# First-layer weights: two VectorE operations a tile through PSUM, the low word's bits from ScalarE

## The chip, the cores and the metric

The kernel runs on one core of one Trainium2 chip. The metric is the device time of one execution in microseconds; less is better. The engines have short names in all rows: PE is TensorE's matmuls, PEld its weight loads, DVE is VectorE, ACT ScalarE, POOL GpSimd, SP SyncE (which here only issues DMAs).

## The reference

Attention in two parts (a pooled one over groups of four positions, and a local band), then two feed-forward layers over 2304 tokens of 512. The layers' weights arrive as 64-bit floats; q, k and v as 32-bit ones.

```python
def _attn_ref(q, k, v):                      # 4 batches, 8 heads, 576 positions, 64 wide
    q_d = q.reshape(B, H, Sd, factor, D).mean(axis=3)
    ...
    out_d = sm_attn(q_d, k_d, v_d)
    out_up = np.repeat(out_d, factor, axis=2)
    mask = np.abs(pos[:, None] - pos[None, :]) < factor
    ...
    return out_up + out_local

def _moe_ref(x, w_in, w_out):                # w_in 512 x 2048, w_out 2048 x 512
    h = x @ w_in
    g = np.where(h > 0.0, h, np.exp(np.minimum(h, 0.0)) - 1.0)
    return g @ w_out

def _moe2_ref(x, w_gate, w_val, w_out):      # 1536 wide
    g = x @ w_gate
    silu = g * (1.0 / (1.0 + np.exp(-g)))
    return silu * (x @ w_val) @ w_out
```

## The kernel before

A planner inside the kernel (class Work) orders everything: each piece of work is a task with an engine, a cost, a due time, the tiles that it reads and writes, and optional earlier tasks (after). When an engine is free in the planner's clock, it takes the ready task that is due first and whose tiles have room. What comes out is one fixed queue for each engine; on the chip each engine works through its queue in order and waits where a semaphore isn't set. So costs and due times move the order, not the chip's durations.

The first layer runs over eight chunks of 288 tokens (T1), three attention units of 96 positions each; batch b fills chunks 2b and 2b+1. In a chunk there are 16 steps f: gemm1 (x by w_in's column block f) into bank 6 or 7, an activation that gives g, and gemm2 (g by w_out's row block f) into banks 0 to 3. Chunk 0 (add_whole, L702) multiplies in plain f32: L713 is gemm1, L718 gemm2 (in the trace the four matmuls of one of these products are eight rows), ScalarE makes e at L723 and L724, VectorE g at L725. Chunks 1 to 7 use split weights and activations, each as a high and a low part in a faster format, three products for each (L688 to L690), with e and g at L757 to L768.

The weights come as pairs of 32-bit words of 64-bit floats. A tile is 128 partitions by 512 numbers, 512 KB of raw words (load_w); the first layer has 32 of them, w_in and w_out for each f. add_words (L341) makes 32-bit floats u of them:

- size (L344, ScalarE): the high word, read as f32, times a power of two, into u. That brings the exponent to the narrower format.
- words_a (L348, VectorE): u shifted left by three bits.
- words_b (L352 and L354, VectorE): the sign bit of the high word or-ed into u, then the low word shifted right by 29 or-ed into u.

The same three steps serve the second layer's weights (add_weights_away), in halves of 256 columns that pass through the tile mid and are written back to DRAM (wd), from the end of chunk 0 on. add_weight_split (L392) makes the two parts for chunks 1 to 7: a cast on ScalarE or VectorE (copy, L275 and L277), then the difference on GpSimd (L400).

Attention for batch 0 runs before chunk 0, for batches 1 to 3 beside the chunks ahead of those that need them. A unit (add_unit) transposes q and k on TensorE (L474), takes scores (L501), a softmax on VectorE, ScalarE and GpSimd, and values (L555); add_pooled does the pooled part of a batch in four pieces (praw are its rows of v, summed at L578 and L579); add_split puts both together as x (L666 to L676). Attention takes its PSUM banks from att_bank: any of the eight at first, and only 4 and 5 once the first layer's products have begun.

All tiles of weights share 33 places of SBUF: raw words in places 19 to 32, u in halves of places 0 to 18, split weights in any that is free. So a raw tile is loaded when a place is free.

Of the kernel before, what the change touches and what calls it, by code (L numbers as in the profile page):

```python
# [9 lines left out]
F32 = mybir.dt.float32  # L10
F32R = mybir.dt.float32r
BF16 = mybir.dt.bfloat16
I32 = mybir.dt.int32
AF = mybir.ActivationFunctionType
ALU = mybir.AluOpType
X = mybir.AxisListType.X
# [2 lines left out]
P = 128  # L19
# [10 lines left out]
UPC = 3  # L30
# [26 lines left out]
class Half(Buf):  # L57
# [5 lines left out]
    t = property(lambda self: False if self.whole.t is None else self.whole.t[:, self.i])  # L63
# [56 lines left out]
class Work:  # L120
# [18 lines left out]
    def add(self, engine, cost, due, fn, reads=(), writes=(), after=(), nbytes=0, second=None, slack=0.0):  # L139
        t = self.Task()  # L140
        t.slack = slack
        t.costs = {engine: cost} if isinstance(engine, str) else dict(zip(engine, cost))
        t.due, t.fn, t.nbytes = due, fn, nbytes
        t.bufs = list(dict.fromkeys([*reads, *writes]))
        t.next, t.left = [], 0
        for d in dict.fromkeys([*after, *(w for b in reads for w in b.writers)]):
            d.next.append(t)
            t.left += 1
        for b in t.bufs:
            b.left += 1  # L150
        for b in writes:
            b.writers.append(t)
        self.made += 1
        second = self.SECOND if second is None else second
        t.key = {e: (t.due + i * second * ("act" in t.costs), self.made) for i, e in enumerate(t.costs)}
        for e in t.costs:
            self.ready.setdefault(e, [])
        if not t.left:
            self.offer(t)
        return t  # L160
# [67 lines left out]
def attention_moe_moe(ctx: ExitStack, tc: tile.TileContext, q, k, v, w_in, w_out, w_gate, w_val, w_o2, ident_in, mask_in, band_in, picks_in, out):  # L228
    nc = tc.nc
# [5 lines left out]
    NF1, NF2 = FF1 // P, FF2 // P  # L235
    HALF = G // 2
    scale = 1.0 / float(D) ** 0.5
    NU = S // U
# [9 lines left out]
    NW = 2 * NF1 + 1  # L248
    U0, U1 = 6, 19
# [35 lines left out]
    add = work.add  # L285
# [3 lines left out]
    w_raws = Places(lambda i: pairs(pools["w"].tile([P, 1024], I32, tag=f"w{i}", name="w")), NW)  # L289
# [4 lines left out]
    begun = []  # L294
    banks = Places(lambda i: pools["ps"].tile([P, 512], F32, tag=f"bank{i}", name="bank"), 8)

    def att_bank():
        return banks.new(lambda: [4, 5] if begun else [4, 5, 6, 0, 1, 2, 3, 7])

    def bank(*places):  # L300
        return banks.new(lambda: places)
# [5 lines left out]
    EAGER, URGENT, SLACK = 15.0, 14.0, 1.0  # L307
# [13 lines left out]
    BIAS = (1023 - 127) // 8  # L321
# [19 lines left out]
    def add_words(due, raw, u, reads=()):  # L341

        def size():
            nc.scalar.mul(u.t.bitcast(F32), raw.t[:, :, 1].bitcast(F32), 2.0 ** -BIAS)  # L344

        def words_a():
            t = u.t.bitcast(I32)
            nc.vector.tensor_scalar(out=t, in0=t, scalar1=3, scalar2=None, op0=ALU.logical_shift_left)  # L348

        def words_b():  # L350
            t = u.t.bitcast(I32)
            nc.vector.scalar_tensor_tensor(  # L352
                out=t, in0=raw.t[:, :, 1], scalar=-0x80000000, op0=ALU.bitwise_and, in1=t, op1=ALU.bitwise_or)
            nc.vector.scalar_tensor_tensor(  # L354
                out=t, in0=raw.t[:, :, 0], scalar=29, op0=ALU.logical_shift_right, in1=t, op1=ALU.bitwise_or)

        part = 0.5 if isinstance(raw.room, Places) and raw.room is not w_raws else 1.0
        add("act", 0.69 * part, due - 4, size, reads=[raw, *reads], writes=[u])
        add("dve", 0.6 * part, due - 3, words_a, reads=[u], writes=[u])
        return add("dve", 1.8 * part, due - 2.5, words_b, reads=[raw, u], writes=[u])  # L360

    def add_weights(keys, dues, whole):

        made = {}
        for n, key in enumerate(keys):
            raw, w = w_raws.new(lambda: range(NW - 1, U1 - 1, -1)), whole(n)
            add("sp", 0.5, dues[n] - 36.0, lambda key=key, raw=raw: load_w(key, raw.t), writes=[raw], nbytes=P * 4096)
            made[key] = add_words(dues[n], raw, w, [w.whole])
            ww[key] = w
        return made  # L370

# [69 lines left out]

    sums = {}

    def add_unit(n, due, load_due, rows=None, after=()):

        b, i = divmod(n, NU)
        q0 = i * U
# [21 lines left out]
        for which, t, dst, count, start, own in ((0, tq, qT, U, 0, 0), (1, tk, kT, KU, PAD, off)):  # L469
            pt = att_bank()  # L470

            def turn(t=t, count=count, pt=pt):
                for p in range(NP):
                    nc.tensor.transpose(pt.t[:, p * count:(p + 1) * count], t.t[:count, p * P:(p + 1) * P], ident[:count, :count])  # L474

            def keep(engine, dst=dst, count=count, start=start, pt=pt):
                copy(engine, dst.t[:, :, start:start + count], pt.t[:, :NP * count].rearrange("p (a t) -> p a t", a=NP))

            half = half_ring.new()

            def pool(engine, which=which, dst=dst, own=own, half=half):
                x = dst.t[:, :, own:own + U].rearrange("p a (g r) -> p a g r", r=R)
                to = sums[b].t[:, which, :, i * GU:(i + 1) * GU]
                if engine == "dve":
                    nc.vector.tensor_reduce(out=to, in_=x, op=ALU.add, axis=X)
                else:
                    nc.gpsimd.tensor_tensor(out=half.t, in0=x[:, :, :, :2], in1=x[:, :, :, 2:], op=ALU.add)
                    nc.gpsimd.tensor_tensor(out=to, in0=half.t[:, :, :, 0], in1=half.t[:, :, :, 1], op=ALU.add)

            add("pe", 0.4, due - EAGER, turn, reads=[t], writes=[pt, dst], slack=SLACK)  # L490
            add(COPIER, (0.5, 0.55), due + 1, keep, reads=[pt], writes=[dst], second=1)
            add(EITHER, (0.56, 1.1), due + 2, pool, reads=[dst], writes=[sums[b], half])

        sc = [att_bank(), att_bank()]

        def scores():
            for p in range(NP):
# [359 lines left out]
    with tc.manual_schedule():  # L857
# [33 lines left out]

        xfs = {}
        for n in range(NU):
            xfs[n] = add_unit(n, 4.0 * n, -40 + 2 * n, rows=(*rows[n], vals[n]))
            if n == 0:
                load_mask()
        for p in range(NP):
# [16 lines left out]
        for b in range(1, B):  # L914
            lo, hi = (time1(s) for s in spans[b])
            for i in range(NU):
                due = lo + (hi - lo) * i / NU
                xfs[b * NU + i] = add_unit(b * NU + i, due, due - 18, after=[words["in", 10 if b == 1 else NF1 - 1]])
            for p in range(NP):
                add_pooled(b, p, hi + 2 * p, hi - 20 + 2 * p)  # L920
            while split < (b + 1) * NU and split // UPC < NC:
                if split // NU == b or xdT[split // NU] is not None:
                    made += [add_split(split, xfs[split], time1(NF1 * (split // UPC)) - 12.0)]
                split += 1
# [70 lines left out]
```

## Time and profile before

| | us |
|---|---|
| median of 3 runs (lowest, highest) | 1056.06 (1055.63, 1056.79) |
| profiled execution, its own time | 1057.0 |
| profiled execution, span | 1055.2 |
| TensorE busy | 1003.8 (95%) |
| VectorE busy | 547.3 (52%) |
| ScalarE busy | 395.6 (37%) |
| GpSimd busy | 344.9 (33%) |

The profiled execution is one run with the hardware profiler on; its own time is the span and 1.8 us around it, and 0.94 us above the median. Shares are means over the whole span: the 95% of TensorE hold for a kernel with a front part (attention and chunk 0, up to about 165 us) and a long part of split products.

### The profile page before, as it was taken

What the parts mean: (1) busy time and instruction counts of PE and PEld (TensorE: products, weight loads), DVE (VectorE), ACT (ScalarE), POOL (GpSimd) and SP (SyncE); (2) the same over time, 40 slices, a digit from 0 to 9 for tenths busy, and PEclk for the clock granted to TensorE, in tenths of its full rate; (3) what the DMA queues carried; (4) which work ended last, traced back from release to release, by engine and by line L of the source; (5) the groups of instructions that cost most, each with busy time, mean ns of one, the idle gap of its engine ahead of it and who ended that gap; (6) DMA issues with size and microseconds to landing.
All of it is one profiled execution on the core that took longest, in us unless ns stands there. A gap on an engine that the chain in (4) does not pass through costs nothing. (4 is left out here: it accounts for less than half of the span.)

```text
span 1055.2 us, 19383 instructions
## 1 busy us (share of the span) xinstructions
PE 1003.8 (95%) x7540; PEld 869.6 (82%) x7540; DVE 547.3 (52%) x1088; ACT 395.6 (37%) x972; POOL 344.9 (33%) x390
## 2 busy tenths in 40 slices
PE   7768979999999999999999999999999999999998
PEld 4556758989999899899998888888888888888897
DVE  4899998886787877873123422222223222222232
ACT  4553546555555465555343531121112111211121
POOL 4475685373344634347347830010001000100000
PEclk7569989999999999999999999999999999999999
DMA  9966516455554476433114420011002000100010
GB/s 155 279 214 185 124 30 154 116 146 150 147 148 122 131 193 160 119 84 100 33 34 129 140 73 21 1 41 41 1 1 65 6 1 1 50 1 1 1 40 21
DMA packets 129004, 91.20 MB, mean 86 GB/s; under 512 B 73744, under 2 KB 116880, under 8 KB 128912
## 3 DMA queue, kind: packets, MB, share of 16 engines
q1 hardware_dynamic: 128768, 89.70, 31.6%
q8 instruction: 59, 0.97, 0.4%
q14 instruction: 33, 0.27, 0.1%
q10 hardware_dynamic: 144, 0.26, 0.1%
HBM read 71.06 MB, written 18.87 MB: 85 GB/s over the span
## 5 line engine op out<-in xcount | busy, mean ns | idle before, releaser
L688 PE MATMUL bank<-x,w 128*128 128x288 f32 (+2 forms) x928 | 317.0, 342 | 8.4 <-DVE e L761 8.3
L689 PE MATMUL bank<-x,w 128*128 128x288 f32 (+2 forms) x928 | 310.9, 335 | 0.1
L690 PE MATMUL bank<-x,w 128*128 128x288 f32 (+2 forms) x928 | 309.9, 334 | 0.0
L834 DVE TENSOR_TENSOR e<-bank,e 128x512 f32<-128x512 f32 (+1 forms) x120 | 76.2, 637 | 260.8 <-ACT e L831 179.3
L688 PEld LDWEIGHTS bank<-x,w 128*128 128x128 f32 x928 | 174.3, 188 | 32.7 <-DVE e L761 12.3
L689 PEld LDWEIGHTS bank<-x,w 128*128 128x128 f32 x928 | 174.9, 188 | 17.0 <-POOL x L676 0.3
L690 PEld LDWEIGHTS bank<-x,w 128*128 128x128 f32 x928 | 174.7, 188 | 16.8
L768 POOL TENSOR_TENSOR g<-e,g 128x288 fp32r<-128x288 f32 x112 | 94.0, 840 | 167.7 <-ACT g L275 117.0
L688 PE MATMUL bank<-g,w 128*128 128x288 f32 x448 | 134.9, 301 | 1.6 <-DVE o L277 1.6
L689 PE MATMUL bank<-g,w 128*128 128x288 f32 x448 | 132.2, 295 | 0.0
L690 PE MATMUL bank<-g,w 128*128 128x288 f32 x448 | 131.9, 294 | 0.0
L811 POOL TENSOR_TENSOR x<-x2r,x 128x512 fp32r<-128x512 f32 (+1 forms) x20 | 23.5, 1193 | 270.2 <-ACT x L810 270.2
L831 ACT ACTIVATE e<-bank 128x512 f32<-128x512 f32 (+1 forms) x60 | 33.2, 556 | 190.3 <-PE bank L690 190.3
L836 ACT CAST y<-e 128x512 fp32r<-128x512 f32 (+1 forms) x60 | 34.6, 577 | 154.9 <-DVE e L834 132.9
L761 DVE SCALAR_TENSOR_TENSOR e<-e,bank 128x288 f32<-128x288 f32 x112 | 50.3, 449 | 76.0 <-ACT e L765 66.2
L688 PEld LDWEIGHTS bank<-g,w 128*128 128x128 f32 x448 | 84.1, 188 | 4.1 <-DVE o L277 1.9
L689 PE MATMUL bank<-w,y 128*128 128x512 f32 x216 | 85.7, 397 | 0.0
L688 PE MATMUL bank<-w,y 128*128 128x512 f32 x216 | 85.3, 395 | 0.0
L690 PE MATMUL bank<-w,y 128*128 128x512 f32 x216 | 84.9, 393 | 0.0
L689 PEld LDWEIGHTS bank<-g,w 128*128 128x128 f32 x448 | 84.6, 189 | 0.2
L690 PEld LDWEIGHTS bank<-g,w 128*128 128x128 f32 x448 | 84.5, 189 | 0.0
L757 ACT ACTIVATE e<-bank 128x288 f32<-128x288 f32 x112 | 46.1, 411 | 99.3 <-PE bank L690 73.0
(114 smaller groups left out, 1458.8 us busy)
## 6 DMA issues: line engine op xcount, KB each, us to landing
wd<-mid SPq DMA_DIRECT2D x72, 128.0 KB
u<-wd SPq DMA_DIRECT2D x36, 256.0 KB
w<-in_moe_w_in_dram SPq DMA_DIRECT2D x16, 512.0 KB
w<-in_moe_w_out_dram SPq DMA_DIRECT2D x16, 512.0 KB
w<-in_moe_w_gate_dram SPq DMA_DIRECT2D x24, 256.0 KB
w<-in_moe_w_val_dram SPq DMA_DIRECT2D x24, 256.0 KB
w<-in_moe_w_out_dram SPq DMA_DIRECT2D x24, 256.0 KB
out_dram<-x2r SPq DMA_DIRECT2D x17, 256.0 KB
```

Of the source, the lines that this page charges most:

```text
L688: nc.tensor.matmul(ps, sh, mh, start=first, stop=False)
L689: nc.tensor.matmul(ps, sh, ml, start=False, stop=False)
L690: nc.tensor.matmul(ps, sl, mh, start=False, stop=last)
L757: nc.scalar.activation(e.t, h.t[:, :T1], AF.Relu, scale=-1.0)
L761: nc.vector.scalar_tensor_tensor(out=e.t, in0=e.t, scalar=-1.0, op0=ALU.add, in1=h.t[:, :T1], op1=ALU.max)
L768: add("pool", 0.82, due - URGENT, lambda e=e, g=g: nc.gpsimd.tensor_tensor(out=g.t[:, 1], in0=e.t, in1=g.t[:, 0], op=ALU.subtract), reads= ...
L811: add("pool", 1.3, due, lambda T=T, raw=raw, x=x: nc.gpsimd.tensor_tensor(out=x.t[:, 1, :T], in0=raw.t[:, :T], in1=x.t[:, 0, :T], op=ALU.s ...
L831: add("act", 0.6, due, lambda T=T, e=e, gate=gate: nc.scalar.activation(e.t[:, :T], gate.t[:, :T], AF.Sigmoid), reads=[gate], writes=[e], ...
L834: add("dve", 0.64, due, lambda T=T, e=e, x=x: nc.vector.tensor_tensor(out=e.t[:, :T], in0=x.t[:, :T], in1=e.t[:, :T], op=ALU.mult), reads= ...
L836: add("act", 0.6, due, lambda T=T, e=e, y=y: nc.scalar.copy(y.t[:, 0, :T], e.t[:, :T]), reads=[e], writes=[y])
```

## The change

The first layer's weights no longer go through add_words. add_weights has its own three functions. ScalarE does two operations a tile: rest (L377 of the changed kernel) makes the low word's top three bits, by reading it as an unsigned number, scaling it by 2 to the minus 29 with an offset, and converting to an integer in u; size (L374) writes the scaled high word into a PSUM bank, 4 or 5. VectorE does two: L381 shifts the bank's content left by three and ors the low bits in, in the bank; L383 takes the sign from the high word and ors the bank in, into u.

With that go changes to the order. Attention before chunk 0 has banks 6, 0, 1, 2, 3 and 7 and leaves 4 and 5. Units 4 to 6 of batch 0 (those of chunk 1) have everything behind their transposes due 24 us later in the planner (late). The transposes of batches 1 to 3 wait until the last word tile is done (then). The planner's costs for word operations are changed too: add_words, now for halves only, and the new tasks.

```diff
--- before.py
+++ after.py
@@ -11,6 +11,7 @@
 F32R = mybir.dt.float32r
 BF16 = mybir.dt.bfloat16
 I32 = mybir.dt.int32
+U32 = mybir.dt.uint32
 AF = mybir.ActivationFunctionType
 ALU = mybir.AluOpType
 X = mybir.AxisListType.X
@@ -295,7 +296,7 @@
     banks = Places(lambda i: pools["ps"].tile([P, 512], F32, tag=f"bank{i}", name="bank"), 8)
 
     def att_bank():
-        return banks.new(lambda: [4, 5] if begun else [4, 5, 6, 0, 1, 2, 3, 7])
+        return banks.new(lambda: [4, 5] if begun else [6, 0, 1, 2, 3, 7])
 
     def bank(*places):
         return banks.new(lambda: places)
@@ -354,18 +355,38 @@
             nc.vector.scalar_tensor_tensor(
                 out=t, in0=raw.t[:, :, 0], scalar=29, op0=ALU.logical_shift_right, in1=t, op1=ALU.bitwise_or)
 
-        part = 0.5 if isinstance(raw.room, Places) and raw.room is not w_raws else 1.0
-        add("act", 0.69 * part, due - 4, size, reads=[raw, *reads], writes=[u])
-        add("dve", 0.6 * part, due - 3, words_a, reads=[u], writes=[u])
-        return add("dve", 1.8 * part, due - 2.5, words_b, reads=[raw, u], writes=[u])
+        add("act", 0.36, due - 4, size, reads=[raw, *reads], writes=[u])
+        add("dve", 0.33, due - 3, words_a, reads=[u], writes=[u])
+        return add("dve", 1.0, due - 2.5, words_b, reads=[raw, u], writes=[u])
+
+
+
+    TOP3 = 2.0 ** -29 * (1 - 2.0 ** -20), -0.5 + 2.0 ** -18
 
     def add_weights(keys, dues, whole):
 
         made = {}
         for n, key in enumerate(keys):
-            raw, w = w_raws.new(lambda: range(NW - 1, U1 - 1, -1)), whole(n)
-            add("sp", 0.5, dues[n] - 36.0, lambda key=key, raw=raw: load_w(key, raw.t), writes=[raw], nbytes=P * 4096)
-            made[key] = add_words(dues[n], raw, w, [w.whole])
+            raw, w, ps = w_raws.new(lambda: range(NW - 1, U1 - 1, -1)), whole(n), bank(4, 5)
+            due = dues[n]
+
+            def size(raw=raw, ps=ps):
+                nc.scalar.mul(ps.t, raw.t[:, :, 1].bitcast(F32), 2.0 ** -BIAS)
+
+            def rest(raw=raw, w=w):
+                nc.scalar.activation(w.t.bitcast(I32), raw.t[:, :, 0].bitcast(U32), AF.Copy, bias=TOP3[1], scale=TOP3[0])
+
+            def words(raw=raw, w=w, ps=ps):
+                t, p = w.t.bitcast(I32), ps.t.bitcast(I32)
+                nc.vector.scalar_tensor_tensor(
+                    out=p, in0=p, scalar=3, op0=ALU.logical_shift_left, in1=t, op1=ALU.bitwise_or)
+                nc.vector.scalar_tensor_tensor(
+                    out=t, in0=raw.t[:, :, 1], scalar=-0x80000000, op0=ALU.bitwise_and, in1=p, op1=ALU.bitwise_or)
+
+            add("sp", 0.5, due - 36.0, lambda key=key, raw=raw: load_w(key, raw.t), writes=[raw], nbytes=P * 4096)
+            add("act", 0.69, due - 4, rest, reads=[raw, w.whole], writes=[w])
+            add("act", 0.69, due - 3.5, size, reads=[raw], writes=[ps])
+            made[key] = add("dve", 1.5, due - 2.5, words, reads=[raw, w, ps], writes=[w, ps])
             ww[key] = w
         return made
 
@@ -441,7 +462,7 @@
 
     sums = {}
 
-    def add_unit(n, due, load_due, rows=None, after=()):
+    def add_unit(n, due, load_due, rows=None, after=(), then=(), late=0.0):
 
         b, i = divmod(n, NU)
         q0 = i * U
@@ -487,11 +508,12 @@
                     nc.gpsimd.tensor_tensor(out=half.t, in0=x[:, :, :, :2], in1=x[:, :, :, 2:], op=ALU.add)
                     nc.gpsimd.tensor_tensor(out=to, in0=half.t[:, :, :, 0], in1=half.t[:, :, :, 1], op=ALU.add)
 
-            add("pe", 0.4, due - EAGER, turn, reads=[t], writes=[pt, dst], slack=SLACK)
+            add("pe", 0.4, due - EAGER, turn, reads=[t], writes=[pt, dst], slack=SLACK, after=then)
             add(COPIER, (0.5, 0.55), due + 1, keep, reads=[pt], writes=[dst], second=1)
             add(EITHER, (0.56, 1.1), due + 2, pool, reads=[dst], writes=[sums[b], half])
 
         sc = [att_bank(), att_bank()]
+        due += late
 
         def scores():
             for p in range(NP):
@@ -891,7 +913,7 @@
 
         xfs = {}
         for n in range(NU):
-            xfs[n] = add_unit(n, 4.0 * n, -40 + 2 * n, rows=(*rows[n], vals[n]))
+            xfs[n] = add_unit(n, 4.0 * n, -40 + 2 * n, rows=(*rows[n], vals[n]), late=0.0 if n < UPC else 24.0)
             if n == 0:
                 load_mask()
         for p in range(NP):
@@ -915,7 +937,8 @@
             lo, hi = (time1(s) for s in spans[b])
             for i in range(NU):
                 due = lo + (hi - lo) * i / NU
-                xfs[b * NU + i] = add_unit(b * NU + i, due, due - 18, after=[words["in", 10 if b == 1 else NF1 - 1]])
+                xfs[b * NU + i] = add_unit(b * NU + i, due, due - 18, after=[words["in", 10 if b == 1 else NF1 - 1]],
+                    then=[words["out", NF1 - 1]])
             for p in range(NP):
                 add_pooled(b, p, hi + 2 * p, hi - 20 + 2 * p)
             while split < (b + 1) * NU and split // UPC < NC:
```

How the queues move, at three places. The first is VectorE's queue around the operation that makes x for chunk 0 (L666, now L688), up to the first g of chunk 0 (L725, now L747). Before:

```order
L666 TENSOR_TENSOR x_953<-f_515,xdT_818 128x4x96
L352 SCALAR_TENSOR_TENSOR w_801<-w_579,w_801 128x512
L354 SCALAR_TENSOR_TENSOR w_801<-w_579,w_801 128x512
L348 TENSOR_SCALAR w_801<-w_801 128x512
L348 TENSOR_SCALAR w_873<-w_873 128x512
L352 SCALAR_TENSOR_TENSOR w_801<-w_591,w_801 128x512
L354 SCALAR_TENSOR_TENSOR w_801<-w_591,w_801 128x512
L352 SCALAR_TENSOR_TENSOR w_873<-w_594,w_873 128x512
L354 SCALAR_TENSOR_TENSOR w_873<-w_594,w_873 128x512
L725 SCALAR_TENSOR_TENSOR g_1019<-e_1003,bank_980 128x288
```

and now:

```order
L688 TENSOR_TENSOR x_969<-f_512,xdT_802 128x4x96
L688 TENSOR_TENSOR x_969<-f_596,xdT_802 128x4x96
L381 SCALAR_TENSOR_TENSOR bank_967<-bank_967,w_917 128x512
L383 SCALAR_TENSOR_TENSOR w_917<-w_605,bank_967 128x512
L381 SCALAR_TENSOR_TENSOR bank_974<-bank_974,w_962 128x512
L383 SCALAR_TENSOR_TENSOR w_962<-w_611,bank_974 128x512
L381 SCALAR_TENSOR_TENSOR bank_1007<-bank_1007,w_962 128x512
L383 SCALAR_TENSOR_TENSOR w_962<-w_619,bank_1007 128x512
L747 SCALAR_TENSOR_TENSOR g_1029<-e_1015,bank_995 128x288
```

Two of x's three parts are on VectorE now, one before. Each w with a number is one half or place of weights. Ahead of x stand four finished tiles before and seven now; ahead of the first g seven before and ten now.

The second is GpSimd's queue ahead of chunk 0, around the sums over praw (L578 and L579, now L600 and L601) and x. Before:

```order
L618 TENSOR_TENSOR pr<-pr,su 72x576
L578 TENSOR_TENSOR praw<-praw 72x2x128
L579 TENSOR_TENSOR vs<-praw 72x128
L578 TENSOR_TENSOR praw<-praw 72x2x128
L579 TENSOR_TENSOR vs<-praw 72x128
L666 TENSOR_TENSOR x<-f,xdT 128x4x96 x2
L666 TENSOR_TENSOR f<-f,xdT 128x384 x3
```

and now:

```order
L640 TENSOR_TENSOR pr<-pr,su 72x576 x2
L421 TENSOR_TENSOR w<-w 128x512 x2
L600 TENSOR_TENSOR praw<-praw 72x2x128
L601 TENSOR_TENSOR vs<-praw 72x128
L600 TENSOR_TENSOR praw<-praw 72x2x128
L601 TENSOR_TENSOR vs<-praw 72x128
L688 TENSOR_TENSOR x<-f,xdT 128x4x96
L688 TENSOR_TENSOR f<-f,xdT 128x384 x3
```

Two splits (L400, now L421) come ahead of the sums; one part of x is gone.

The third is TensorE's queue where chunk 2 begins: the last second products of chunk 1 (bank from g), attention of batch 2, and the first product of chunk 2 (bank from x). Before:

```order
L690 MATMUL bank<-g,w 128x288
L555 MATMUL bank<-bd,vrows 64x96 x8
L474 MATMUL bank<-ident,rows 128x112 x4
L474 MATMUL bank<-ident,rows 128x96 x4
L688 MATMUL bank<-x,w 128x288
```

and now:

```order
L712 MATMUL bank<-g,w 128x288
L523 MATMUL bank<-kT,qT 32x32 x32
L577 MATMUL bank<-bd,vrows 64x96 x8
L495 MATMUL bank<-ident,rows 128x96 x4
L495 MATMUL bank<-ident,rows 128x112 x4
L523 MATMUL bank<-kT,qT 32x32 x32
L710 MATMUL bank<-x,w 128x288
```

Five pieces of batch 2's attention stand between now, three before.

## Rows read from the trace of the kernel before

**Rows 1.** Windows: busy us by engine, granted PE clock, DMA share, GB/s.

```profile
core 0: us, PE busy (x) PEld busy (x) DVE busy (x) ACT busy (x) POOL busy (x), PEclk, DMA share, GB/s
56.00:157.00 101.00, 80.14 (x532) 59.37 (x531) 96.69 (x124) 49.15 (x102) 70.41 (x62) 0.88 0.48 131
...
74.00:90.60 16.60, 12.05 (x48) 8.83 (x48) 16.46 (x16) 7.71 (x16) 14.52 (x11) 1.00 0.43 128
...
118.00:140.70 22.70, 15.57 (x196) 11.57 (x193) 22.39 (x31) 12.22 (x28) 21.74 (x21) 0.97 0.38 80
140.70:157.00 16.30, 14.59 (x139) 10.45 (x140) 14.69 (x22) 6.98 (x15) 13.20 (x11) 0.84 0.13 29
...
166.00:200.00 34.00, 34.00 (x411) 31.63 (x410) 28.25 (x76) 20.84 (x64) 13.11 (x18) 1.00 0.56 145
...
220.00:240.00 20.00, 18.29 (x265) 16.34 (x264) 18.53 (x35) 9.57 (x24) 17.00 (x21) 1.00 0.73 179
```

**Rows 2.** Groups, 0 to 200 us: busy us, mean ns, idle before and its releasers.

```profile
L713 PE MATMUL bank<-x,w 128*128 128x288 f32 x128 | 40.4, 467 | 19.8 <-DVE w L354 11.6 <-POOL x L666 5.4 <-DVE g L725 2.8
L352 DVE SCALAR_TENSOR_TENSOR w<-w 128x512 int32<-128x512 int32 x32 | 37.7, 1178 | 0.0
L354 DVE SCALAR_TENSOR_TENSOR w<-w 128x512 int32<-128x512 int32 x32 | 34.4, 1074 | 1.1
L718 PE MATMUL bank<-g,w 128*128 128x288 f32 x128 | 34.3, 412 | 0.6 <-DVE w L354 0.6
...
L348 DVE TENSOR_SCALAR w<-w 128x512 int32<-128x512 int32 x32 | 23.2, 749 | 0.0
L344 ACT ACTIVATE w<-w 128x512 f32<-128x512 f32 x32 | 21.1, 672 | 11.4 <-DMA w<-in_moe_w_in_dram 4.2 <-DMA w<-in_moe_w_out_dram 4.1 <-POOL w L400 1.5
```

**Rows 3.** Timeline of TensorE: start, us, instructions, idle before and its releaser.

```profile
65.58 6.77 PE L713 MATMUL bank<-x,w 128*128 128x288 f32 x16 [5.41 <-POOL x L666]
...
90.66 3.53 PE L713 MATMUL bank<-x,w 128*128 128x288 f32 x8 [3.36 <-DVE w L354]
...
102.16 4.04 PE L718 MATMUL bank<-g,w 128*128 128x288 f32 x16
...
117.67 0.50 PE L474 MATMUL bank<-ident,rows 96*128 96x96 f32 x4
...
140.70 4.21 PE L713 MATMUL bank<-x,w 128*128 128x288 f32 x8 [5.23 <-DVE w L354]
...
159.40 1.01 PE L474 MATMUL bank<-ident,rows 112*128 112x112 f32 x8 [0.89 <-DVE f L277]
```

**Rows 4.** Single lines, 0 to 200 us: ns min/median/max, first and last start.

```profile
L352 DVE SCALAR_TENSOR_TENSOR w<-w x32: 657/684/7242, 49.1 to 155.0; 128x512 int32<-128x512 int32 x32
...
L354 DVE SCALAR_TENSOR_TENSOR w<-w x32: 691/850/1656, 49.8 to 156.4; 128x512 int32<-128x512 int32 x32
...
L725 DVE SCALAR_TENSOR_TENSOR g<-e,bank x16: 436/442/454, 73.4 to 159.9; 128x288 f32<-128x288 f32 x16
```

**Rows 5.** Timeline of VectorE, the longest word operation.

```profile
63.48 7.24 DVE L352 SCALAR_TENSOR_TENSOR w<-w 128x512 int32<-128x512 int32 x1
```

**Rows 6.** Timeline of GpSimd around it.

```profile
60.80 0.75 POOL L578 TENSOR_TENSOR praw<-praw 72x256 f32<-72x256 f32 x1 [5.51 <-DMA praw<-in_v_dram]
...
63.83 1.69 POOL L666 TENSOR_TENSOR x<-f,xdT 128x384 f32<-128x384 f32 x2
...
68.91 1.26 POOL L400 TENSOR_TENSOR w<-w 128x512 fp32r<-128x512 f32 x1
```

**Rows 7.** Groups by form, whole span, VectorE.

```profile
L834 DVE TENSOR_TENSOR e<-bank,e 128x512 f32<-128x512 f32 x96 | 66.0, 690 | 233.5 <-ACT e L831 158.2 <-PE bank L690 75.3
...
L837 DVE TENSOR_TENSOR y<-e,y 128x512 fp32r<-128x512 f32 x48 | 33.1, 692 | 39.1 <-ACT y L836 39.0
```

**Rows 8.** Batch 1's attention: chunk 2's first product, VectorE's word group, the window.

```profile
232.22 0.38 PE L688 MATMUL bank<-x,w 128*128 128x288 f32 x1
...
L352 DVE SCALAR_TENSOR_TENSOR w<-w 128x512 int32<-128x512 int32 x10 | 11.7, 1172 | 0.0
...
117.67:232.22 114.55, 104.19 (x1182) 89.76 (x1180) 99.37 (x202) 64.15 (x177) 73.11 (x79) 0.97 0.44 109
```

## The prediction

> **What bounds the kernel now.** The windows by stage come first [rows 1]. From 166 us on TensorE works nearly all the time (34.00 of 34.00 us), with small holes such as the 1.71 us between 220 and 240. Before that it doesn't: from 56 to 157 us it is busy 80.14 of 101 us, while VectorE is busy 96.69 of them, 16.46 of 16.60 and 22.39 of 22.70 in two stretches of chunk 0. So VectorE bounds chunk 0, and TensorE bounds what follows. A microsecond saved in chunk 0 moves the end only if the later part doesn't then wait for something else.
>
> TensorE's groups say what chunk 0's products wait for [rows 2]: 11.6 + 0.6 us for the last word operation of a tile (L354) and 2.8 us for g, 15.0 us together; the 5.4 us for x lie ahead of chunk 0. Its timeline has the two longest of these waits, 3.36 and 5.23 us [rows 3], and 0.89 us more at a transpose that waits for a copy on VectorE.
>
> What VectorE does there stands in its groups [rows 2]: 749 + 1178 + 1074 ns = 3.00 us a tile, 96 us for 32. The spread matters more than the mean [rows 4]: L352 takes 657 ns at least and 7242 at most, L354 691 to 1656; but L725, with one input in a PSUM bank and one in SBUF, takes 436 to 454 ns, always. The 7.24 us instance starts at 63.48 and ends at 70.72 [rows 5], and GpSimd works on without a gap from 60.80 to 70.17 [rows 6]. So an operation of VectorE with both inputs in SBUF stands still while GpSimd works, and one with an input from PSUM doesn't.
>
> **The words of the first layer.** Three operations a tile become two, each with one SBUF input and one from PSUM, 128x512. No row has this form. The nearest: L834 (bank and SBUF, 128x512, f32) takes 690 ns, L837 (both in SBUF, on a stretch with little GpSimd work) 692 [rows 7]. I take 0.69 us an operation, since L725 shows that the bank keeps it flat, and 1.38 a tile. The low end is 0.66 (L352's minimum); the high end is 1.13, the mean of L352's and L354's means, as if GpSimd still stopped it. At 0.69 the 32 tiles cost 44 us where they cost 96: VectorE is freed of 52 us before 158 us. Both ends are kept for the range.
>
> [...]
>
> **ScalarE** gets one more operation a tile, for the low word, at the 672 ns of L344 [rows 2]: 21.5 us over 32 tiles. It was busy 49.15 of 101 us [rows 1], so the sum of 71 fits. I cost it at nothing; without that cover it is up to 21.5 us.
>
> **Where chunk 0 starts.** Its first product waits for x until 65.58 [rows 3]. GpSimd waits 5.51 us for the DMA of praw, until 60.80, sums four pieces of it, and makes two parts of x in 1.69 us [rows 6]. In the new order VectorE makes two parts and GpSimd one: -0.8 us. Two splits now stand ahead of those sums on GpSimd; the 5.51 us of waiting cover their 2 x 1.3. Attention ahead of chunk 0 has six banks instead of eight, and VectorE has seven tiles instead of four ahead of x; the same wait for praw and the four sums (until 63.83) cover that, or else it costs what it is late. SP's queue is the same up to the first two praw loads; the later ones slip behind a few weights, and a weight's slot comes free when its tile is done, no later than before.
>
> **Inside chunk 0.** VectorE has ten tiles done ahead of chunk 0's first g (seven before), and then two tiles and one g a step: 2 x 1.38 + 0.44 = 3.2 us. TensorE needs 4.0 a step (two products of 8 rows in 4.04 us [rows 3]). So the waits should nearly all go, 15.0 + 0.9 = 15.9 us, of which I leave 2 for single late g's. Slow matmuls go with the holes: behind 3.36 us of waiting a product took 3.53 us, behind 5.23 us 4.21, against 4.04 / 2 = 2.02 at full clock [rows 3]. That is 1.5 + 2.2 us, of which I take 3.3 (1.3 + 2.0), since a single product's row holds the tail of its last matmul too. [...] The slow first 16 rows (6.77 us) stay.
>
> **The held transposes.** Batch 1's transposes now wait for the last word tile of all. They stand in TensorE's queue ahead of the 13th first-layer product, so a late word stops everything behind them. TensorE reaches them after 22 products: 64.8 + 6.8 + 20 x 2.02 = 112 us. On VectorE the last tile stands ahead of the 12th g, so it is done at about 107 to 110. I cost the hold at nothing; each microsecond that the words are late costs one.
>
> **What is late next: chunk 2.** Batch 1's attention must be ready when chunk 2 starts. Its first transpose ran at 117.67 [rows 3] and chunk 2's first product at 232.22 [rows 8]: 114.5 us, of which TensorE spent 104.19 busy and, of these, 2.0 in slow matmuls. With full work it would have 102 us. VectorE was busy 99.37 us [rows 8]. Ten tiles of words lie in it, 30 us, which go; thirteen casts of weights come to it from ScalarE, 9 us at L837's 0.69 [rows 7]. That leaves 78 of 102 us, a lighter share than 99 of 114. Still, the chain of small operations may be too long, and the new order gives TensorE five pieces of batch 2 ahead of chunk 2's first product instead of three, work to fill a wait. I take 4 us, between 0 and 12 (attention keeps its 114.5 us).
>
> **Sum.** 0.8 + 15.9 + 3.3 = 20.0 us, less 2 and less 4: 14.0. Against the profiled execution's 1057.0 us that is 1043.0; the median of the runs shown is 0.94 lower, so **1042.1 us**. Later stages keep their TensorE work, and their VectorE has room.
>
> **Rivals.**
> 1. Attention becomes the bound: chunk 2 keeps its 114.5 us from the first transposes. The gain is 20.0 - 2 - 12 = 6, so 1050. For it: VectorE at 87% there, and two banks for all of attention; against it: 21 us of VectorE's work leave that stretch.
> 2. More: no wait is left in chunk 0 and the 1.7 us at 220 to 240 us go too: 20.0 + 1.7 = 21.7, so 1034.4.
> 3. Nothing: GpSimd still stops the new operations, 1.13 us each. The 22 tiles left when chunk 0 starts, with 12 g, take 22 x 2.26 + 12 x 0.44 = 55 us, the first ten end some 9 us later than at 66, and the last word comes at 130 us. The held transposes stop TensorE until then, 12 us later than 117.67, which eats what was won ahead: 1055 to 1058.
> 4. Slower: the two banks don't overlap. Each tile then runs one thing after another, 2 x 0.67 on ScalarE, 1.38 on VectorE and some 0.2 of hand-over, 2.92 us, with each step's e and g (three operations of 288 columns like L725, 1.3 us) between. 22 tiles and 12 steps take 22 x 2.92 + 12 x 1.3 = 80 us, the last word comes at 146, and TensorE stands until then: 28 us later than 117.67, less the 12 lost afterwards now, 16 us slower, about 1072. It decides where the last word comes after 130 us. Against it: ScalarE's queue has writes to both banks one behind the other, so that one fills while the other is worked on.
>
> **Numbers.** The forecast (1036 to 1046) 0.60; rival 1 (1046 to 1052) 0.19; rival 2 (1030 to 1036) 0.10; rival 3 0.05; rival 4 0.06. Faster by over 0.2% (about what a measurement can tell from no change) 0.89, within it 0.05, slower 0.06. The range leaves out rivals 3 and 4 and the outer ends of 1 and 2: 1034 to 1050.
>
> **What would show it.** Right: both new operations at 0.65 to 0.72 us with no long ones; under 3 us of waits for words in chunk 0; batch 1's first transpose at about 112 us and chunk 2's first product at 213 to 221 instead of 232.2. Wrong: new operations of over 1 us; TensorE waiting at batch 1's first transposes; a hole of over 8 us ahead of chunk 2, which is rival 1.

## The result and the profile after

| | before | after |
|---|---|---|
| median of the runs, us | 1055.85 (1054.36 to 1056.79, 4 runs) | 1040.63 (1037.42 to 1043.80, 4 runs) |
| ratio, 95% interval | | 0.9857 [0.9824, 0.989] |
| profiled execution, own time | 1057.0 | 1041.44 |
| its span | 1055.2 | 1039.6 |
| VectorE busy | 547.3 | 526.0 |
| ScalarE busy | 395.6 | 404.1 |
| GpSimd busy | 344.9 | 318.4 |

The change is faster by 15.2 us; 1042.1 was forecast, with 1034 to 1050.

The groups of the kernel after, from 0 to 200 us, answer to [rows 2] (busy us, mean ns, idle before and what ended it).

```profile
L735 PE MATMUL bank<-x,w 128*128 128x288 f32 x128 | 37.4, 441 | 7.5 <-POOL x L688 4.9 <-DVE g L747 2.6
...
L381 DVE SCALAR_TENSOR_TENSOR bank<-bank,w 128x512 int32<-128x512 int32 x32 | 22.1, 692 | 1.2 <-ACT bank L374 1.1
L383 DVE SCALAR_TENSOR_TENSOR w<-w,bank 128x512 int32<-128x512 int32 x32 | 22.0, 688 | 1.1
...
L377 ACT ACTIVATE w<-w 128x512 int32<-128x512 uint32 x32 | 20.7, 669 | 1.0 <-DMA w<-in_moe_w_in_dram 1.0
L374 ACT ACTIVATE bank<-w 128x512 f32<-128x512 f32 x32 | 20.0, 634 | 0.3 <-DVE w L383 0.3
```

A tile costs VectorE 1.38 us instead of 3.00. No product waits for a word any more: of 12.2 us nothing is left, and 2.6 us of waiting for g remain beside the 4.9 ahead of chunk 0. The single lines of both operations answer to [rows 4] (ns min/median/max, first and last start).

```profile
L381 DVE SCALAR_TENSOR_TENSOR bank<-bank,w x32: 665/693/700, 41.3 to 103.4; 128x512 int32<-128x512 int32 x32
...
L383 DVE SCALAR_TENSOR_TENSOR w<-w,bank x32: 686/689/689, 42.0 to 104.1; 128x512 int32<-128x512 int32 x32
```

They are flat where L352 went up to 7.24 us, and the last word starts at 104.1 us instead of 156.4. The windows (as in [rows 1]; the second one is batch 1's attention, as the last row of [rows 8]) show where TensorE still stands.

```profile
core 0: us, PE busy (x) PEld busy (x) DVE busy (x) ACT busy (x) POOL busy (x), PEclk, DMA share, GB/s
56.00:157.00 101.00, 91.82 (x782) 72.54 (x779) 86.45 (x159) 62.34 (x136) 59.55 (x61) 0.94 0.56 152
...
106.31:217.39 111.08, 103.08 (x1241) 89.76 (x1239) 93.21 (x196) 55.28 (x159) 72.17 (x77) 0.96 0.42 106
...
200.00:220.00 20.00, 16.28 (x239) 14.68 (x238) 17.74 (x33) 7.09 (x19) 14.89 (x21) 0.80 0.75 181
```

Chunk 0's stretch is fuller (91.82 us busy against 80.14), but a new hole stands between 200 and 220 us, with a granted clock of 0.80 in the mean: 1.00 from 200 to 210 us, 0.65 from 210 to 217.39, where the waits are, and 0.50 from there to 220. TensorE's timeline names the places, as in [rows 3].

```profile
61.33 8.29 PE L735 MATMUL bank<-x,w 128*128 128x288 f32 x24 [4.90 <-POOL x L688]
...
106.31 0.88 PE L495 MATMUL bank<-ident,rows 96*128 96x96 f32 x8
109.17 3.63 PE L735 MATMUL bank<-x,w 128*128 128x288 f32 x8 [1.97 <-DVE g L747]
...
212.33 1.55 PE L577 MATMUL bank<-bd,vrows 128*64 128x96 f32 x16 [2.87 <-DVE sm L535]
...
217.39 0.61 PE L710 MATMUL bank<-x,w 128*128 128x288 f32 x1
```

Three times divide the span: chunk 0's first product, batch 1's first transposes (106.31) and chunk 2's first product (217.39). Before, the last two were 117.67 and 232.22. So 11.4 us were won ahead of the transposes, 3.5 between there and chunk 2 (111.08 us against 114.55), and 0.8 behind it: together the 15.6 by which the spans differ. These three times are also the best summary of all runs. Each is read from one trace, whose time lies up to 2.4 us from the median of its kernel.

| kernel | median us | ratio | chunk 0 | first transposes | chunk 2 | transposes to chunk 2 | chunk 2 to end |
|---|---|---|---|---|---|---|---|
| before | 1055.85 | | 65.6 | 117.7 | 232.2 | 114.6 | 823.0 |
| after | 1040.63 | 0.9857 | 61.3 | 106.3 | 217.4 | 111.1 | 822.2 |
| two operations, SBUF | 1048.14 | 0.9934 | 67.5 | 112.6 | 226.5 | 113.9 | 820.0 |
| three operations, bank | 1053.75 | 0.9993 | 62.4 | 119.0 | 229.4 | 110.4 | 821.9 |
| three operations, SBUF | 1060.53 | 1.0047 | 68.0 | 123.4 | 238.7 | 115.3 | 820.3 |
| words alone | 1033.18 | 0.9791 | 64.8 | 104.8 | 211.4 | 106.7 | 821.6 |
| without the hold | 1033.58 | 0.9797 | 61.5 | 100.6 | 206.5 | 105.9 | 823.9 |
| without the 24 us | 1046.96 | 0.9919 | 64.7 | 108.7 | 219.5 | 110.8 | 827.0 |
| eight banks | 1032.16 | 0.978 | 58.0 | 105.3 | 206.9 | 101.6 | 821.1 |
| six banks only | 1038.49 | 0.984 | 63.8 | 105.9 | 210.0 | 104.1 | 827.7 |
| batch 2 held | 1042.97 | 0.9886 | 61.7 | 106.7 | 208.6 | 101.9 | 832.6 |
| praw held | 1033.69 | 0.9807 | 57.7 | 102.5 | 207.1 | 104.6 | 822.7 |
| praw held, no hold | 1030.58 | 0.9767 | 58.2 | 97.9 | 204.8 | 106.9 | 825.0 |
| words alone, praw held | 1030.24 | 0.978 | 59.6 | 103.6 | 205.6 | 102.1 | 822.1 |

Most of what differs between them is settled when chunk 2 starts, after 204.8 to 238.7 us: from there to the end every kernel but one takes 820 to 828 us. The rows from "words alone" on belong to the experiments with the order, below.

### The profile page after: what moved, and what is told of

The parts are those of the page before. It is cut to its first block, busy times and chain, and to the rows that moved or that the text cites. A ratio compares the mean times of both kernels' runs of the same rounds, so it can differ in the third digit from the quotient of the medians.

```text
span 1039.6 us, 19385 instructions
## 1 busy us (share of the span) xinstructions
PE 998.2 (96%) x7540; PEld 870.3 (84%) x7540; DVE 526.0 (51%) x1080; ACT 404.1 (39%) x994; POOL 318.4 (31%) x375
```

## Experiments: two operations or the bank

Four kernels with the same queues on every engine but for these operations: two or three operations of VectorE, in SBUF or in the bank. The first keeps both operations in SBUF. Not shown here: ScalarE's product is also placed behind its low-word operation, since it now overwrites the low words which that one reads.

```diff
 def size(...):
-    nc.scalar.mul(ps.t, raw.t[:, :, 1].bitcast(F32), 2.0 ** -BIAS)
+    nc.scalar.mul(raw.t[:, :, 0].bitcast(F32), raw.t[:, :, 1].bitcast(F32), 2.0 ** -BIAS)
...
 def words(...):
-    t, p = w.t.bitcast(I32), ps.t.bitcast(I32)
+    t, p = w.t.bitcast(I32), raw.t[:, :, 0]
```

> The changed kernel with the same two operations of VectorE a tile and the same order on every engine, but the product of ScalarE goes to the low words' place in SBUF instead of a PSUM bank, so both inputs of VectorE lie in SBUF. My theory (an operation with both inputs in SBUF is stopped while GpSimd works, one with an input in a bank is not): the two operations have a mean of 0.95 to 1.2 us between 41 and 104 us, single ones over 2 us, GpSimd's subtraction for the weights' low part goes back from 1.29 to about 1.5 us, the last word is late for batch 1's first transposes, and the time is 1046 to 1056. Rival (it is only that there are two operations instead of three): both stay at 0.69 us, the time within 3 us of the changed kernel's 1040.6.

Measured: 1048.14 us (1047.28 to 1050.01, 6 runs), ratio 0.9934 [0.9921, 0.9947]. Its single lines, and the longest instance on VectorE's timeline with GpSimd's beside it:

```profile
L381 DVE SCALAR_TENSOR_TENSOR w<-w x32: 675/686/3424, 43.8 to 111.5; 128x512 int32<-128x512 int32 x32
...
L383 DVE SCALAR_TENSOR_TENSOR w<-w x32: 691/694/3982, 44.7 to 113.0; 128x512 int32<-128x512 int32 x32
...
54.42 3.98 DVE L383 SCALAR_TENSOR_TENSOR w<-w 128x512 int32<-128x512 int32 x1
...
53.28 2.11 POOL L640 TENSOR_TENSOR pr<-pr,su 72x576 f32<-72x576 f32 x1 [0.98 <-DMA w<-in_moe_w_in_dram]
55.36 2.50 POOL L421 TENSOR_TENSOR w<-w 128x512 fp32r<-128x512 f32 x2
```

The shortest are as short as in the bank, so the bank isn't faster in itself; the longest lies beside GpSimd's operations for 3.44 of its 3.98 us. All 64 instances say the same. In the changed kernel 13 of them have GpSimd busy over nine tenths of their time, and none of these takes more than 0.70 us; with both inputs in SBUF 14 have, and they take 0.68 to 1.77 us, 1.18 in the mean. Where GpSimd is idle (36 in each kernel) both kernels have 0.68 to 0.70. So the theory holds, in the time too. Two details of it don't: the mean of L381 is 0.90 us, under the range (L383's is 1.00), and GpSimd's subtraction has a median of 1.33 us, not 1.5. The new order keeps GpSimd idle in much of the words' time (2.39 us busy from 74 to 90 in this kernel, 14.52 of 16.60 before [rows 1]), so less is stopped than before the change even in SBUF.

What the bank is worth lies mostly ahead of chunk 0, where GpSimd works: chunk 0 starts at 61.3 with it and at 67.5 without. In SBUF VectorE's two parts of x stand behind a long word operation; in the bank they start at 55.18.

```profile
62.30 3.42 DVE L381 SCALAR_TENSOR_TENSOR w<-w 128x512 int32<-128x512 int32 x1
...
66.37 1.02 DVE L688 TENSOR_TENSOR x<-f,xdT 128x384 f32<-128x384 f32 x2
```

The other two rows of the square take the three old operations, in the bank and in SBUF, and leave out ScalarE's operation for the low word. Their lines are L381 (shift), L382 (sign) and L384 (low bits), and all that follows is one line further down.

```diff
 def words(...):
...
+    u, t = ps.t.bitcast(I32), w.t.bitcast(I32)
+    nc.vector.tensor_scalar(out=u, in0=u, scalar1=3, scalar2=None, op0=ALU.logical_shift_left)
+    nc.vector.scalar_tensor_tensor(
+        out=u, in0=raw.t[:, :, 1], scalar=-0x80000000, op0=ALU.bitwise_and, in1=u, op1=ALU.bitwise_or)
+    nc.vector.scalar_tensor_tensor(
+        out=t, in0=raw.t[:, :, 0], scalar=29, op0=ALU.logical_shift_right, in1=u, op1=ALU.bitwise_or)
```

> The changed kernel's order and banks, with three operations of VectorE a tile as before, worked in the PSUM bank (the shift in the bank, the sign into the bank, the low bits from the bank to SBUF); ScalarE's operation for the low bits is left out. My theory: all three stay flat at 0.65 to 0.75 us, so a tile costs 2.1 us on VectorE instead of 1.38, two tiles and a g 4.6 us against TensorE's 3.9 a step: chunk 0 is bound by VectorE by some 0.7 us a step for ten steps, and the time is 1044 to 1050, clearly better than before. Rival (the number of operations does it, not where they lie): 1052 to 1057.

> The changed kernel's order and banks with before's three operations of VectorE in SBUF; ScalarE's operation for the low bits is left out. My theory: 2.7 to 3.1 us a tile with single operations of several us; the last word comes at 135 to 155 us and batch 1's held transposes with all of TensorE's queue wait for it; 1056 to 1070, no gain from the order alone. Rival (the order is what pays): 1040 to 1046.

For the second, u is w.t and ScalarE writes the product there. Measured: 1053.75 us in the bank (1051.65 to 1057.43, 12 runs, 0.9993 [0.9981, 1.0005]), 1060.53 in SBUF (1058.79 to 1061.67, 6 runs, 1.0047 [1.0033, 1.0061]). Single lines, first in the bank, then in SBUF:

```profile
L381 DVE TENSOR_SCALAR bank<-bank x32: 664/692/693, 41.4 to 116.8; 128x512 int32<-128x512 int32 x32
...
L382 DVE SCALAR_TENSOR_TENSOR bank<-w,bank x32: 695/697/697, 42.1 to 117.6; 128x512 int32<-128x512 int32 x32
...
L384 DVE SCALAR_TENSOR_TENSOR w<-w,bank x32: 686/686/687, 42.9 to 118.3; 128x512 int32<-128x512 int32 x32
```

```profile
L381 DVE TENSOR_SCALAR w<-w x32: 391/420/1082, 42.1 to 123.6; 128x512 int32<-128x512 int32 x32
...
L382 DVE SCALAR_TENSOR_TENSOR w<-w x32: 691/692/3970, 42.8 to 124.1; 128x512 int32<-128x512 int32 x32
...
L384 DVE SCALAR_TENSOR_TENSOR w<-w x32: 691/692/1645, 43.9 to 124.8; 128x512 int32<-128x512 int32 x32
```

In the bank all three are flat, as expected, but the time lies 3.8 us above the range, inside the rival's (1052 to 1057). That rival, which says that the place doesn't matter, falls by the other row: the same three operations cost 6.8 us more in SBUF. I had counted 0.7 us a step against the changed kernel. Chunk 0 also starts 1.1 us later; TensorE then waits 7.4 us for g up to its 22nd product, and 2.4 us more at batch 1's first transposes, with all of its queue behind them:

```profile
119.03 0.94 PE L496 MATMUL bank<-ident,rows 96*128 96x96 f32 x8 [2.40 <-DVE w L384]
```

That wait is not the hold (then), which moves the planner's queues and sets no wait on the chip. With two operations in SBUF the transposes start at 112.59, while the last word ends at 114.6. By the code it is the bank: the transposes write bank 4 or 5, and L384 still reads the last tile there.

The transposes come 12.7 us later than in the changed kernel, and 12.0 of these come through to chunk 2 (229.4 against 217.4). In SBUF the time is in its range, but a tile costs VectorE 2.30 us and not 2.7 to 3.1, the last word ends at 126.4 and not at 135 or later, and the transposes don't wait for it.

So the two parts add up, as far as the noise tells (the changed kernel's interval is 3.5 us to either side): the bank is worth 6.8 us with three operations and 7.5 with two, the third operation (without ScalarE's) 12.4 in SBUF and 13.1 in the bank. The order alone, with the old operations, costs 5.4 (1060.53 against the 1055.17 of before, run beside it).

## Experiments: the three settings of the order

Each undoes one or more of them: the hold (then), the 24 us (late), and the six banks.

```diff
-        return banks.new(lambda: [4, 5] if begun else [6, 0, 1, 2, 3, 7])
+        return banks.new(lambda: [4, 5] if begun else [4, 5, 6, 0, 1, 2, 3, 7])
...
-            xfs[n] = add_unit(n, 4.0 * n, -40 + 2 * n, rows=(*rows[n], vals[n]), late=0.0 if n < UPC else 24.0)
+            xfs[n] = add_unit(n, 4.0 * n, -40 + 2 * n, rows=(*rows[n], vals[n]), late=0.0)
...
-                    then=[words["out", NF1 - 1]])
+                    )
```

All three undone:

> The two operations through the bank and their ScalarE operation, with the three settings of the order undone: batch 1's transposes are not held, batch 0's last three units are not put off by 24 us, and attention ahead of chunk 0 may use all eight banks. My theory: the words are worth nearly all of the gain: 1038 to 1047, with waits for words in chunk 0 of a few us at most because attention's instructions stand between them on VectorE. Rival (the order is needed, since attention holds the two banks that the words need and VectorE's queue): 1048 to 1056.

Measured: 1033.18 us (1031.38 to 1034.87, 4 runs), 0.9791 [0.9772, 0.9809]; the interval doesn't meet that of the change. That is 4.8 us under my range, which had put the words at nearly the gain of the whole. The words, with their costs in the planner, are worth 22.0 us, and the settings give 7.4 of them back. Then each of them undone by itself, and last all but the six banks:

> The changed kernel with one setting of the order undone: batch 1's first transposes are no longer held for the last word tile (the 24 us for batch 0's last units and the six banks stay). The words alone gave 1033.2, so the three settings together cost 7.4 us; the changed kernel's trace puts a hole of 3.7 us and slow matmuls ahead of chunk 2's first product, where values and scores of a later unit stand in TensorE's queue. Theory H (the hold starts batch 1 late, so that its last unit stands ahead of chunk 2): 1033 to 1036, chunk 2's first product before 213 us without a hole. Rival L (the 24 us do it) or B (the six banks do it): 1038 to 1042.

> The changed kernel with the 24 us for batch 0's last units undone (hold and six banks stay). Theory H (the hold): no gain, 1038 to 1043. Rival L (the 24 us put batch 0's last units where batch 1's belong and so push those behind): 1033 to 1036.

> The changed kernel with attention ahead of chunk 0 on eight banks again (hold and 24 us stay). Theory H: chunk 0 starts up to 3.4 us later, as with the words alone (64.8 against 61.3), and that costs up to as much: 1040 to 1044. Rival B (the six banks cost time later on): 1034 to 1038.

> The words through the bank with the six banks for attention ahead of chunk 0, without the hold and without the 24 us. Theory H: chunk 0 starts at about 61 us and chunk 2 without a hole, so both gains add up: 1029 to 1033. Rival (the start of chunk 0 is not worth anything, since batch 1's attention sets when chunk 2 starts): 1033 to 1036, as with the words alone.

Measured: without the hold 1033.58 (0.9797 [0.9784, 0.981]); without the 24 us 1046.96 (0.9919 [0.9906, 0.9932]); with eight banks 1032.16 (0.978 [0.9764, 0.9795]); six banks alone 1038.49 (0.984 [0.9823, 0.9857]). Theory H gives the first number and misses the others, and the time without the 24 us (1046.96) lies above both ranges. With eight banks and the hold kept, chunk 0 starts earlier, at 57.95, where H had it later, and chunk 2 comes 101.6 us after the transposes, with TensorE busy for 96.75 of them; that is under B's range too. With the six banks alone chunk 0 starts at 63.8, not 61, and the time is above both ranges.

The differences between these kernels give each setting a price. The six banks cost 5.3 us by themselves (1038.49 against 1033.18) and 8.5 beside the other two (1040.63 against 1032.16). Where the six banks stand, the hold costs 7.1 us with the 24 us and 8.5 without, and the 24 us gain 6.3 with the hold and 4.9 without. With eight banks the hold and the 24 us together cost nothing (1032.16 against 1033.18); each alone there wasn't run. So neither the hold nor the banks is the cause by itself. Each setting moves the planner's whole order, and these are the prices in this order only. The kernels at 1034 us or less reach chunk 2 at 204.8 to 211.4 us; the one with the six banks alone does too, but takes 827.7 us from there.

**What stands ahead of chunk 2.** In the change, values (L577 at 212.33) and scores of later units stand in the queue there. Here the planner holds batch 2's transposes until chunk 2's x is made (batch 3's until chunk 4's); every order is the same until shortly before.

```diff
-                    then=[words["out", NF1 - 1]])
+                    then=[words["out", NF1 - 1]] if b == 1 else made[UPC * 2 * (b - 1):][:UPC])
```

> The changed kernel with batch 2's transposes (and batch 3's) held until the parts of x of chunk 2 (chunk 4) are made; every engine's order is the same until just ahead of chunk 2. Theory: in the changed kernel x of chunk 2 is complete at about 213 us, but its first product starts at 217.4, since scores and values of a later unit wait in TensorE's queue ahead of it; without them it starts at 211 to 214 us, and since the time from there to the end was 820 to 828 us in every kernel so far, the time is 1034 to 1038. Rival (the later pieces only fill a wait that chunk 2 has anyway, or batch 2 is then late for chunk 4): 1039 to 1044.

Measured: 1042.97 us (1041.23 to 1045.44, 5 runs), 0.9886 [0.9865, 0.9907], no gain: the rival holds. Chunk 2's first product starts at 208.59, and the next one waits for x:

```profile
214.34 0.61 PE L711 MATMUL bank<-x,w 128*128 128x288 f32 x1 [5.35 <-POOL x L698]
```

So in the changed kernel's order the later pieces fill a wait that x makes anyway. Here x comes some 3 us ahead of the changed kernel's start of chunk 2 (217.39), but from there to the end it takes longer (1041.2 less 214.34 is 826.9 us, against 822.2); that the pieces taken out must be done later fits, but wasn't traced. What was late was mostly batch 1's chain up to x, not the queue.

**Why chunk 0 starts when it does.** GpSimd's timeline in the changed kernel, which answers to [rows 6]:

```profile
58.00 0.72 POOL L600 TENSOR_TENSOR praw<-praw 72x256 f32<-72x256 f32 x1 [4.94 <-DMA praw<-in_v_dram]
...
60.42 0.86 POOL L688 TENSOR_TENSOR x<-f,xdT 128x384 f32<-128x384 f32 x1
```

These praw are rows of v of batch 1: batch 0's lie in tiles named w. They are needed long after chunk 0 starts. By its rule the planner put them ahead of x because they were ready in its clock and x wasn't. (With eight banks the order has x ahead of them, and there chunk 0 starts at 57.95.) The edit holds, in the planner, their loads, and so their sums, until w_in's eleventh tile (the 21st of all) is done.

```diff
-                add_pooled(b, p, hi + 2 * p, hi - 20 + 2 * p)
+                add_pooled(b, p, hi + 2 * p, hi - 20 + 2 * p, after=[words["in", 10 if b == 1 else NF1 - 1]])
...
-                out=t.t, in_=rows_of("v", b, u, 2 * p, 2 * p + 2)), writes=[t], nbytes=HALF * 2048 * 1.2)
+                out=t.t, in_=rows_of("v", b, u, 2 * p, 2 * p + 2)), writes=[t], nbytes=HALF * 2048 * 1.2, after=after)
```

> The changed kernel with batch 1's loads and sums of praw held until the eleventh word tile is done, as its other loads are. In the changed kernel GpSimd waits 4.94 us for that DMA until 58.0 and sums four pieces ahead of its part of batch 0's x. Theory S: GpSimd reaches its part of x with no wait for a DMA, chunk 0 starts at 54 to 58 us instead of 61.3; with it the order ahead of chunk 2 has no later unit's scores in it, chunk 2 starts before 212 us, and the time is 1030 to 1036. Rival (the start is bound by batch 0's own attention or the sums are then in the way of the weights): chunk 0 starts at 60 to 62 us, the time is 1037 to 1043.

> As before it, but without the hold of batch 1's transposes: the words through the bank, the six banks, the 24 us, and praw of batch 1 held. If what chunk 0 gains at its start and what the missing hold gains add up, chunk 0 starts at 54 to 58 us, chunk 2 at 202 to 206, and the time is 1027 to 1031. If batch 1's chain of small operations sets when chunk 2 starts: as without the hold alone, 1032 to 1035.

> The words through the bank with none of the three settings of the order, and batch 1's loads and sums of praw held until the eleventh word tile is done. If the three settings are worth something once the sums no longer stand ahead of x: 1033 or more, as the words alone (1033.2). If holding the sums does by itself what the settings were for: chunk 0 starts at 54 to 59 us instead of 64.8, chunk 2 before 209, and the time is 1027 to 1032, the same as the best so far (1030.6).

Measured: on the change 1033.69 us (1031.62 to 1037.73, 5 runs), 0.9807 [0.9785, 0.983]; without the hold 1030.58 (1028.98 to 1031.55, 4 runs), 0.9767 [0.9749, 0.9785]; on the words alone 1030.24 (1029.46 to 1032.48, 5 runs), 0.978 [0.9765, 0.9795]. GpSimd and TensorE in the first of them:

```profile
55.16 0.87 POOL L688 TENSOR_TENSOR x<-f,xdT 128x384 f32<-128x384 f32 x1 [1.85 <-ACT xdT L276]
...
57.74 8.05 PE L735 MATMUL bank<-x,w 128*128 128x288 f32 x24 [1.05 <-DVE x L688]
```

No DMA is waited for, chunk 0 starts 3.6 us earlier, and theory S holds. In the traces chunk 2 comes 10.3 us earlier (6.5 of them between the transposes and chunk 2, where the order changed with it); the medians differ by 6.9. Without the hold the gains add up as expected (chunk 0 at 58.2, chunk 2 at 204.8). On the words alone chunk 0 starts at 59.6, where 54 to 59 was expected, and the time is in the range.

With praw held the three settings are worth nothing that shows: 1030.2 without any, 1033.7 with all. But on the words alone holding praw gains little that is clear of noise either: a ratio of 0.978 against 0.9791, with intervals that overlap. The two best kernels can't be told apart, nor can the one with eight banks (0.978); the one without the settings is the simpler, at 0.978 of the time before.

## Why the prediction was right, step by step

**The new operations: right.** 0.69 us taken, 0.692 and 0.688 measured, none over 0.70. The reason is shown by the square: the same two operations in SBUF, with the same queues, reach 3.98 us beside GpSimd and cost 7.5 us of the time. Rivals 3 and 4 needed long operations or banks that don't overlap; the last word came at 104.8, not at 130 or 146. Rival 4's 0.2 us of hand-over a tile was an estimate; in the trace after, L374 ends at 101.63 us and L381, which waits for it, starts at 101.67. In itself the bank costs these two operations nothing that shows: medians of 693 and 689 ns with it, 686 and 694 without.

**ScalarE: right in size** (20.7 us taken by L377 against 21.5), and no product waits for it. A run that takes only this operation away wasn't made.

**The start: wrong in size.** "-0.8 us" became -4.25 (65.58 to 61.33). I held GpSimd's wait for praw for fixed. The DMA landed 2.80 us earlier (58.00 against 60.80), the sums took 2.42 us instead of 3.03, and one part of x instead of two saved 0.83. What made the transfer land earlier wasn't separated: its queue position and the traffic ahead both differ. The same order with the two operations in SBUF starts chunk 0 at 67.53, later than before, so none of this comes without the bank; I had put the bank's worth inside chunk 0. I had also read "a wait for praw" without asking whose rows they are.

**Chunk 0: right.** 15.9 us of waits less 2 was the forecast; 2.6 us of waits for g are left and none for words. The products ran 1.94 us apart (19 of them from 69.45 to 106.31), as they did in the kernel before (1.93, two from 102.16 to 106.03). The 2.02 that I took was half of a row that ends with its last matmul's tail, 0.09 us too much, which is 1.8 us over 20.

**"I cost the hold at nothing": the step that failed**, together with the six banks, which I also put at nothing (covered by the wait for praw), and the 4 us for what is late next. The transposes came at 106.31 (112 forecast), but from there chunk 2 took 111.08 us, where 102 + 4 = 106 was forecast. That is rival 1's mechanism, at three quarters of its price (9.1 us of 12 over the 102). In the stretch TensorE stands 8.0 us (111.08 less 103.08) and has slow products behind the waits (a row of 3.63 us at 109.17, at a granted clock of 0.59, against rows of 2.10 at 1.00 from 69.45 to 106.31). Taking back the hold gives batch 1 a start 5.8 us earlier and gains 7.1 us; taking back the six banks instead gains 8.5, with the hold in place. I had the way of it wrong too: no late word stops TensorE at the transposes (nothing is waited for at 106.31), since the hold acts only in the planner. What it does is put batch 1 later in the queues.

Part of the cost is VectorE's queue. I forecast 78 us of work for VectorE in that stretch; it was 93.21. The casts took 11.9 us for twelve, not 9 for thirteen, and the softmax's multiplications and subtractions (sm) came over from GpSimd, 10.4 us instead of 2.9. The casts behind the last words, as seen on VectorE (first their group in the whole stretch) and GpSimd:

```profile
L278 DVE CAST w<-w 128x512 fp32r<-128x512 f32 x12 | 11.9, 1013 | 1.2 <-POOL w L421 1.2
...
104.70 4.05 DVE L278 CAST w<-w 128x512 fp32r<-128x512 f32 x3
108.67 0.44 DVE L747 SCALAR_TENSOR_TENSOR g<-e,bank 128x288 f32<-128x288 f32 x1
...
103.13 13.80 POOL L421 TENSOR_TENSOR w<-w 128x512 fp32r<-128x512 f32 x10 [2.02 <-DVE w L383]
```

I took 0.69 us a cast; these three beside GpSimd take 1.35 each, and g, which stands behind them, is 1.97 us late.

**The sum held by luck, because two errors met:** 3.4 us more at the start and 2.2 in chunk 0's products and slow start, against 5.1 less behind the transposes; 0.8 came after chunk 2's start, where nothing was forecast. The forecast for the profiled execution was 1043.0, measured 1041.44.

**Left open:** through which instructions the 24 us help and the six banks cost (by themselves they show behind chunk 2's start, 827.7 us to the end instead of 821.6) wasn't traced.

## What to carry to other kernels

Where two engines stop each other, as VectorE and GpSimd do here (a word operation takes up to 3.98 us in SBUF and 0.70 at most in the bank), moving one operand to PSUM can pay (7.5 us here) even if the operation gets no faster in itself, and here its gain added to that of taking an operation away: measure the two in a square with the order held fixed. Cost changes of the order as parts of their own; here they took back a third of what the new words gained, and asking whose data a waiting engine waits for brought about as much back on the changed kernel. In a kernel ordered by a planner, find the one time that the end hangs on (here chunk 2's first product) and read every variant by it.

## What the runs showed that was not expected

- A cast of VectorE with a single SBUF input can be stopped by GpSimd too: in the kernel after, the casts of the weights' parts (128x512) take up to 1.50 us beside GpSimd's subtractions (at 105.84), but not every time (0.49 at 112.48), and 0.41 to 0.42 with GpSimd idle (at 94.65, 125.03 and 139.37).
- In the two kernels with three operations the shift by a constant has a median of 420 ns in SBUF and 692 in the bank, while the operations with two inputs have 692 in SBUF, 697 and 686 in the bank. So the bank costs the one-input operation 0.27 us here.
- GpSimd gains as well: its subtraction for the weights' low part has a median of 1286 ns after, 1538 before, 1330 with two operations in SBUF.
